# Zero products of other widths, and pooled maxima moved up, in a fused attention, bilinear and SoLU kernel

## The chip, the cores and the metric

The kernel runs on one core of a Trainium2 chip. The time is device microseconds of one execution; 735.52 us is the median of three runs (735.33 to 736.11).

The engines that matter: TensorE (PE, matrix products; loads of its stationary operand are shown as PEld), VectorE (DVE), ScalarE (ACT), GpSimd (POOL), and SyncE (SP), which issues nearly all DMAs. Each engine works through its instructions in order.

## The reference

Attention with 4 batches, 8 heads, 576 positions and head size 64 gives the sum of two parts. Its output, 2304 tokens of 512, goes through a bilinear layer and then a SoLU layer. All is fp32.

```python
def sm_attn(qq, kk, vv):
    s = scale * np.matmul(qq, kk.transpose(0, 1, 3, 2))
    s = s - np.max(s, axis=-1, keepdims=True)
    a = np.exp(s)
    a = a / (np.sum(a, axis=-1, keepdims=True) + 1e-09)
    return np.matmul(a, vv)
# pooled part: q, k, v averaged over 4 positions, attended, each row repeated 4 times
out_up = np.repeat(sm_attn(q_d, k_d, v_d), 4, axis=2)
# local part: only |i - j| < 4 counts
out_local = ...
x = out_up + out_local                # 2304 x 512
x = ((x @ w_a) * (x @ w_b)) @ w_out   # d_ff 1536
h = x @ w_in                          # d_ff 1024
solu = h * softmax(h)
out = (layernorm(solu) * g_ln) @ w_out2
```

## The kernel before

**Stages.** Tokens are taken in five blocks of 512 (the last has 256). The bilinear layer of a block runs in 12 chunks of 128 hidden columns: chunk c has a first product `A0`, a second product `A1` (12 passes each, `emit_A`), their elementwise product on DVE (`emit_mult`), its split into a high and a low half on ACT and DVE (`emit_p`), and the out product `B` (12 passes, `emit_B`), which is issued one chunk later. While a block runs, the attention of the next block is computed between its products. The attention of block 0 has no cover and runs alone at the start, some 44 us. The SoLU layer comes last.

**Splitting.** Products with 512 columns use a high and a low half of each operand, three passes for each: high x high, high x low, low x high. The weights arrive as 64-bit words and go through five steps, `w{i}.1` to `w{i}.5` (`w_stages`): two ACT instructions, a shift and an add on DVE (lines 142 and 145), a rounding on ACT (line 153), and the low half on DVE (line 160). Step 5 gives the operand of a chunk's third pass.

**Attention items.** A pooled head pair, `p{b}_{hp}`, has: sums of q and k over four positions on DVE (`qsum0`, `qsum1`, line 262), scores on PE (line 286), maxima on DVE (line 296), exponentials on ACT, normalising of E (`norm`; in block 1 all on DVE, line 335), transposes on PE (`ptr`, line 368), their copy on ACT (`pte`), the value product (`pvm`), its copy. A local unit, `l{s}` (128 tokens), has scores (line 468), maxima, exponentials (line 508), sums and scaling on DVE (`norm`, lines 517 to 528), transposes and a value product. In block 0 the local transposes are PE's (line 559); for later units DVE transposes 32 x 32 tiles (`turn32`, line 535), which SP writes to DRAM and reads back turned (`place`). Scores, transposes and value products of both kinds share the two PSUM banks `x0` and `x1`.

**Order.** For block 0 the order is written out, in `FIRST`, and is fixed on every engine. After that, items are put on a time line with `add(t, item)`, in units of which one chunk has four, and `advance(t)` issues all with a smaller time. It is called at 4c + 1.33 (between `A0` and `A1`), at 4c + 2.67 (behind the multiply) and at 4c + 4 (behind the out product of chunk c - 1). In the chunks of block 0 every engine keeps the order of issue (`pin(None)`). `p_at` and `l_at` give the times of pooled and local items of block 1 within a head pair's stretch, eight thirds of a chunk long; p1_0 to p1_3 and l4 to l7 are the items that run beside block 0's chunks.

**Zero products.** `fill` issues products of zeros into a PSUM tile that real work will overwrite. `FILL` gives how many, by place: `S0`, `S1`, `S2` ahead of the pooled scores of the first three head pairs of block 0, `pv2` ahead of the third pooled value product, `lS3`, `lPT0_0` and `lo3_0` ahead of the scores of unit 3, the first transposes of unit 0 and the value product of unit 3. All have 128 columns.

Of the kernel before, what the change touches and what calls it, by code (L numbers as in the profile page):

```python
# [17 lines left out]
B, H, S, D = 4, 8, 576, 64  # L18
# [9 lines left out]
NCH = FF1 // 128  # L28
EDGES = [8, 9, 13, 17]
NBOOT = NSUB  # L30
FILL = dict(S0=10, S1=12, S2=10, pv2=2, lPT0_0=2, lo3_0=2, lS3_0=2, PT2=0)

FIRST = (
# [25 lines left out]
def kernel(  # L59
# [17 lines left out]
    PE, ACT, DVE, POOL, SP = nc.tensor, nc.scalar, nc.vector, nc.gpsimd, nc.sync  # L77
# [106 lines left out]
    zz = base.tile([128, 128], F32, name="zz")  # L184
# [2 lines left out]
    mhalf = base.tile([128, 1], F32, name="mhalf")  # L187

    def fill(key, out):
        for _ in range(FILL.get(key, 0)):  # L190
            PE.matmul(out=out, lhsT=zz[:, 0:out.shape[0]], rhs=zz, start=True, stop=True, skip_group_check=True)


    att, att_ps = ExitStack(), ExitStack()
# [43 lines left out]
    def pooled_items(b, hp):  # L238
        i = b * NP + hp
        st = {}  # L240
# [33 lines left out]
        def scores():  # L274
            if b:
                st["S"] = [aps.tile([R, 2 * SD], F32, tag=f"x{e}", name="S") for e in range(2)]
            elif hp % 2 == 0:
                t = aps.tile([72, 2, 512], F32, tag="S", name="S")
                st["S"] = [t[:, e, 0:2 * SD] for e in range(2)]
            else:  # L280
                st["S"] = [ps.tile([72, 512], F32, tag=f"acc{e}", name="S")[:, 0:2 * SD] for e in range(2)]
            if not b:
                fill(f"S{hp}", st["S"][0][:, 0:128])
            for half in range(2):
                for e in range(2):
                    PE.matmul(
                        out=st["S"][e][:, half * SD:(half + 1) * SD],
                        lhsT=st["q"][e * 64:e * 64 + 64, half * R:half * R + R],
                        rhs=st["k"][e * 64:e * 64 + 64, :], start=True, stop=True,
                    )  # L290
# [64 lines left out]
        def ptr():  # L355
            if turned:
                return
            if b:
                st["PT"] = [aps.tile([72, 2 * SD], F32, tag=f"x{e}", name="PT") for e in range(2)]
            else:  # L360
                st["PT"] = [ps.tile([72, 512], F32, tag="ab", bufs=2, name="PT")[:, 0:2 * SD] for e in range(2)]
            if not b:
                fill(f"PT{hp}", st["PT"][0][:, 0:128])
            for e in range(2):
                for kh in range(2):
                    for h in range(2):
                        o = kh * SD + h * 72
                        PE.transpose(st["PT"][e][:, o:o + 72], st["E"][:, e, h, kh * 72:kh * 72 + 72],
                                     id_sb[:72, :72])
# [24 lines left out]
        def pve():  # L394
            if b not in up:
# [5 lines left out]
                    vsum=lambda: (vsum2(), vsum1()), smax=smax, exps=exps, norm=lambda: (inverse(), scaled()), ptr=ptr, pte=pte,  # L401
# [31 lines left out]
    def local_items(s):  # L433

        st = {}
# [13 lines left out]
        def scores(hps=range(NP)):  # L449
            if hps[0] == 0:  # L450
                if s in (1, 3):
                    t = aps.tile([128, 2, 512], F32, tag="S", name="lS")
                    st["S"] = [t[:, e] for e in range(2)]
                elif s == 2:
                    st["S"] = [ps.tile([128, 512], F32, tag=f"acc{e}", name="lS") for e in range(2)]
                else:
                    st["S"] = [aps.tile([128, 512], F32, tag=f"x{e}", name="lS") for e in range(2)]
            fill(f"lS{s}_{hps[0]}", st["S"][1][:, 384:512])
            if s < NMASK:
                for e in range(2):  # L460
                    PE.matmul(out=st["S"][e][:, 0:NP * KW].rearrange("p (h k) -> p h k", k=KW), lhsT=id_r,
                              rhs=mk_r[:, kind, :].unsqueeze(1).to_broadcast([128, NP, KW]),
                              start=True, stop=False, skip_group_check=True)
            for hp in hps:
                for n in range(2):
                    for e in range(2):
                        q, k = qk_of(n, hp, e)
                        PE.matmul(out=st["S"][e][n * QW:n * QW + QW, hp * KW:hp * KW + KW], lhsT=q, rhs=k,  # L468
                                  start=s >= NMASK, stop=True, skip_group_check=True)
# [80 lines left out]
        def ptr(half):  # L550
            def f():
                if s == 2:
                    pt_ = ps.tile([KW, 4, 128], F32, tag=f"acc{half}", name="lPT")
                else:
                    pt_ = ps.tile([KW, 4, 128], F32, tag="ab", bufs=2, name="lPT")
                fill(f"lPT{s}_{half}", pt_[:, 0, :])
                for a in range(4):
                    hp, e = 2 * half + a // 2, a % 2
                    PE.transpose(pt_[:, a, :], st["P"][:, NP * e + hp, :], id_sb)
                st["pt", half] = pt_  # L560
            return f
# [10 lines left out]
        def pvm(half):  # L572
            def f():
                if half == 0:
                    if s == 2:
                        st["o"] = aps.tile([128, 2, 512], F32, tag="S", name="lo")[:, 0].rearrange("p (h c) -> p h c", c=128)
                    else:
                        st["o"] = aps.tile([128, NP, 128], F32, tag="x0" if s == 1 else "x1", name="lo")
                fill(f"lo{s}_{half}", st["o"][:, 2 * half, :])
                for hp in (2 * half, 2 * half + 1):  # L580
                    for n in range(2):
                        for e in range(2):
                            c = (2 * hp + e) * D
                            if s > 3:
                                PE.matmul(out=st["o"][e * 64:e * 64 + 64, hp, n * QW:n * QW + QW].rearrange("p (a i) -> p a i", a=2),  # L585
                                          lhsT=st["vw"][n][:, c:c + D], rhs=st["PT"][:, 2 * n:2 * n + 2, NP * e + hp, :],
                                          start=True, stop=True, skip_group_check=True)
                                continue
                            PE.matmul(out=st["o"][e * 64:e * 64 + 64, hp, n * QW:n * QW + QW],
                                      lhsT=st["vw"][n][:, c:c + D],  # L590
                                      rhs=st["PT", half][:, 2 * (hp % 2) + e, n * QW:n * QW + QW],
                                      start=True, stop=True, skip_group_check=True)
            return f
# [12 lines left out]
        cols = slice(s % 4 * 128, s % 4 * 128 + 128)  # L606
# [488 lines left out]
    def add(t, f):  # L1095
        timeline.append((t, seq[0], f))
        seq[0] += 1
# [21 lines left out]
    for n, word in enumerate(FIRST.split()):  # L1119
        key, name = word.split(".")  # L1120
# [2 lines left out]

    QS, LS4 = 2.7, 4
    turn = 8
    p_at = dict(load=-2.5, loadv=-1, qsum0=0.95, qsum1=1.2, scores=2.8, smax=2.9, exps=3.3, vsum=3.5, norm=4.1, ptr=5.8, pte=5.9,
                pvm=6.8, pve=6.9)
    l_at = dict(loadqk=1 - turn, loadv=8.1 - turn, scores=0.8, mask=0.9, smax=0.91, exps=1.1, norm=2.1, turn32=3.4,
                place=3.45, pvm0=7.8, pvm1=7.81, evac=7.9)
# [2 lines left out]
    for blk in range(1, NBLK):  # L1132
        at = lambda r, o: 48 * (blk - 1) + (turn * r + o + (2 if blk == 1 else 0)) * 4 / 3
        for r in range(width[blk] // 128):
            if blk < B:
                for name, f in (pooled_items(blk, r) if blk > 1 else pool1[r]).items():
                    if (blk, r) == (1, 0) and "load" in name:
                        continue
                    if (blk, r) == (1, 0) and "qsum" in name:
                        add(QS + (name == "qsum1") / 100, f)  # L1140
                    else:
                        add(at(r, (q_at if blk > 1 else p_at)[name]), f)
            s = 4 * blk + r
            if s in VECTOR:
                for o, f in vector_items(s):
                    add(at(0, o + (2 + 15 * r if blk == B else turn * r - 3.7)), f)
                continue
            for name, f in locs[s].items():
                if name in l_at and not (s == 4 and "load" in name):
                    add(at(r, l_at[name] + (-0.4 if s > 7 and name == "turn32" else 0.6 if s > 7 and name == "place" else 0)) if s > 4 or l_at[name] > 1 else  # L1150
                        LS4 + l_at[name] / 100, f)
            add(at(r, 9) if blk == B else at(3, (7.2 + 0.3 * r if blk == 1 else 8 + 0.1 * r) if r < 3 else 8.3), locs[s]["split"])
    for i in range(5, 3 * NCH):
# [8 lines left out]
    def at(t, *fs):  # L1162
        for f in fs:
            late.append((t, len(late), f))
# [85 lines left out]
    blk = NBLK - 1  # L1250
# [176 lines left out]
```

## Time and profile before

| | |
|---|---|
| median of three runs | 735.52 us (735.33 to 736.11) |
| profiled execution | 742.58 us, its span 740.8 us |
| busy: PE, PEld, DVE, ACT, POOL | 722.0, 593.3, 455.3, 331.3, 241.5 us |
| instructions | 12089, of them 4478 PE passes and as many loads |
| chain that ended last | PE 68%, DVE 19%, ACT 4%, DMA 4% of the span |

A busy time is a sum over the whole span; a stage can have another limit than the sum shows. PE's share is high because nearly all stages wait for it, so what counts are the few stretches in which it stands still or runs at a lower clock. The granted clock is printed as a share of 2.4 GHz.

### The profile page before, as it was taken

To read this page: it belongs to the slowest core of one execution; us is meant where nothing else is said; L and a number is where in the kernel's file an instruction comes from. 1 tells how busy PE (TensorE), PEld (TensorE's weight loads), DVE (VectorE), ACT (ScalarE), POOL (GpSimd) and SP (SyncE) were. 2 spreads that over 40 slices of the span, in tenths; PEclk is the share of its full clock that TensorE was granted. 3 is DMA by queue.
4 is the path that set the end of the run, shared out by engine and by line. 5 is a ranking of instruction groups with operands and counts; after the bars stand their busy time and mean duration, and the time that the engine had idled before them with its cause. 6 is when DMAs were issued, how large, how long until landed. Compare 5 with 4: busy or idle time off the path is not lost.

```text
span 740.8 us, 12089 instructions
## 1 busy us (share of the span) xinstructions
PE 722.0 (97%) x4478; PEld 593.3 (80%) x4478; DVE 455.3 (61%) x874; ACT 331.3 (45%) x695; POOL 241.5 (33%) x253
## 2 busy tenths in 40 slices
PE   8898989999999999999999999999999999999997
PEld 7686767777788787887788888889898888888886
DVE  6589879887325426335425858749857865656640
ACT  5578677744122214222213111147867655544441
POOL 4410101112324423224311112110038978687332
PEclk9599999999999999999999999999999999999999
DMA  8994875336343324332231120165414554554441
GB/s 240 265 362 173 247 242 170 104 102 184 92 127 121 115 83 130 116 117 80 59 115 57 37 79 18 40 240 165 143 58 143 177 192 143 170 171 142 142 142 58
DMA packets 84275, 102.99 MB, mean 139 GB/s; under 512 B 11032, under 2 KB 65080, under 8 KB 84216
## 3 DMA queue, kind: packets, MB, share of 16 engines
q1 hardware_dynamic: 83672, 102.01, 44.2%
q8 instruction: 35, 0.57, 0.3%
q10 hardware_dynamic: 544, 0.21, 0.2%
q14 instruction: 24, 0.20, 0.1%
HBM read 75.72 MB, written 26.48 MB: 138 GB/s over the span
## 4 chain that ended last, share of the span: by engine, by line
PE 68%; DVE 19%; ACT 4%; DMA 4%; issue 3%; SPq 1%; POOL 0%; DVEq 0%; ACTq 0%; POOLq 0%
PE ab L738 24%; PE o L1083 13%; PE c L963 9%; PE acc L783 6%; PE accS L783 5%; PE c L936 3%; DVE wm L145 2%; DVE vx L687 2%; DVE vpr L685 1%; PE lo L585 1%; DVE wm L142 1%; DVE w L160 1%; PE lS L468 1%; DVE qkds L262 1%; DVE a L751 1%
## 5 line engine op out<-in xcount | busy, mean ns | idle before, releaser
L738 PE MATMUL ab<-xTh,w 128*128 128x512 f32 (+1 forms) x976 | 287.8, 369 | 4.5 <-DVE a L751 2.4
L738 PEld LDWEIGHTS ab<-xTh,w 128*128 128x128 f32 x976 | 176.4, 189 | 38.4 <-DVE w L160 3.5
L738 PE MATMUL ab<-xTl,w 128*128 128x512 f32 (+1 forms) x488 | 178.7, 366 | 0.3 <-DVE xTl L219 0.3
L738 PEld LDWEIGHTS ab<-xTl,w 128*128 128x128 f32 x488 | 92.1, 189 | 14.9 <-DVE xTl L219 1.0
L759 POOL TENSOR_TENSOR pl<-a,ph 128x512 fp32r<-128x512 f32 x36 | 47.2, 1312 | 153.9 <-ACT ph L757 153.9
L751 DVE TENSOR_TENSOR a<-a,ab 128x512 f32<-128x512 f32 (+1 forms) x60 | 37.8, 630 | 92.7 <-PE ab L738 90.3
L783 PE MATMUL acc<-ph,w 128*128 128x512 f32 (+1 forms) x288 | 88.2, 361 | 0.0
L757 ACT CAST ph<-a 128x512 fp32r<-128x512 f32 (+1 forms) x60 | 34.7, 578 | 94.7 <-DVE a L751 93.6
L746 ACT COPY a<-ab 128x512 f32<-128x512 f32 (+1 forms) x60 | 32.5, 542 | 99.5 <-PE ab L738 86.9
L268 POOL TENSOR_TENSOR vp<-vp 72x512 f32<-72x512 f32 x16 | 20.9, 1309 | 146.7 <-DMA vp<-vp 146.7
L783 PE MATMUL accS<-ph,w 128*128 128x512 f32 x192 | 66.9, 389 | 0.0
L783 PEld LDWEIGHTS acc<-ph,w 128*128 128x128 f32 x288 | 51.8, 189 | 9.3 <-issue 1.6
L1083 PE MATMUL o<-w,cTh 128*128 128x512 f32 x192 | 59.1, 389 | 0.0
L835 POOL TENSOR_TENSOR xr<-xr 128x256 f32<-128x256 f32 x28 | 29.6, 1079 | 67.7 <-DMA xr<-o1d 67.1
L783 PE MATMUL acc<-pl,w 128*128 128x512 f32 (+1 forms) x144 | 51.2, 355 | 0.0
L783 PEld LDWEIGHTS accS<-ph,w 128*128 128x128 f32 x192 | 36.0, 188 | 7.7
L1083 PEld LDWEIGHTS o<-w,cTh 128*128 128x128 f32 x192 | 36.0, 188 | 7.4
L1074 POOL TENSOR_TENSOR cTl<-raw,cTh 128x512 fp32r<-128x512 f32 x24 | 34.0, 1435 | 22.4 <-ACT cTh L1072 22.4
L145 DVE CUSTOM_DVE_ANT_0 wm<-raw,wm 128x1024 uint16<-128x1024 uint16 x52 | 37.0, 711 | 2.7
L783 PE MATMUL accS<-pl,w 128*128 128x512 f32 x96 | 37.4, 389 | 0.0
L1083 PE MATMUL o<-w,cTl 128*128 128x512 f32 x96 | 37.3, 389 | 0.0
L137 ACT ACTIVATE raw<-raw 128x512 f32<-128x512 f32 x52 | 35.7, 687 | 0.1
(168 smaller groups left out, 1248.5 us busy)
## 6 DMA issues: line engine op xcount, KB each, us to landing
raw<-w SPq DMA_DIRECT2D x52, 512.0 KB
qkr<-qkp SPq DMA_DIRECT2D x32, 288.0 KB
vd<-v SPq DMA_DIRECT2D x18, 512.0 KB
raw<-vd SPq DMA_DIRECT2D x72, 128.0 KB
vp<-vp SPq DMA_DIRECT2D x16, 288.0 KB
pd<-lT SPq DMA_DIRECT2D x12, 384.0 KB
out<-ob SPq DMA_DIRECT2D x18, 256.0 KB
vw<-vwin SPq DMA_DIRECT2D x32, 140.0 KB
```

Of the source, the lines that this page charges most:

```text
L137: ACT.activation(out=hw, in_=hw, func=AF.Prelu, scale=2.0 ** -112, alpha=2.0 ** 32)
L145: DVE.tensor_tensor(out=st["w"], in0=st["w"], in1=st["low"], op=ALU.add)
L738: PE.matmul(out=abs_[blk, j][n][:, c0:c1], lhsT=w[:, ws], rhs=x[:, k, c0:c1], start=(k == 0 and i == 0), stop=(k == 3 and i == 2), skip_gr ...
L746: ACT.copy(out=a, in_=abs_[blk, j][0])
L751: DVE.tensor_tensor(out=a, in0=a, in1=pb, op=ALU.mult)
L757: ACT.copy(out=ph, in_=a)
L759: low = lambda: (POOL if 0 < blk < NBLK - 1 else DVE).tensor_tensor(out=pl, in0=a, in1=f32(ph), op=ALU.subtract)
L783: PE.matmul(out=accs[blk][m], lhsT=wt[:, ms], rhs=x, start=(j == 0 and i == 0 and (w == WIDE or m % 2 == 0)), stop=(j == NCH - 1 and i == ...
L835: POOL.tensor_tensor(out=at[o], in0=at[m], in1=at[n], op=op)
L963: PE.matmul(out=out, lhsT=xx[:, ks], rhs=w, start=(kt == 0 and q_ == 0 and not more), stop=(kt == 1 and q_ == 2), skip_group_check=True)
L1074: POOL.tensor_tensor(out=h4(lo)[:, k], in0=raw[:, k], in1=f32(h4(hi)[:, k]), op=ALU.subtract)
L1083: PE.matmul(out=o, lhsT=x[:, k, :], rhs=w, start=(k == 0 and q_ == 0), stop=(k == 7 and q_ == 2))
```

## The change

The entries of `FILL` become pairs (number, columns). `S0` goes from 10 products of 128 columns to 28 of 48, `S1` from 12 of 128 to 12 of 64, `S2` from 10 of 128 to 4 of 256. The three places with two products of 128 columns get one of 256, and the two at `pv2` go.

In block 0's chunks the times of pooled items move: scores from 2.8 to 2.0, maxima from 2.9 to 2.05, exponentials from 3.3 to 2.4, normalising from 4.1 to 3.3. The first head pair has times of its own: scores at 7 and maxima at 7.05 (before 6.40 and 6.53), exponentials at 7.6 (before 7.07), normalising at 8.8 (before 8.13). `turn32` and `place` of units 4 to 7 go later by 0.9.

What this does to the order of issue, by item:
- p1_0: scores and maxima go from ahead of `emit_p(0, 1)` to behind the out product of chunk 0; on DVE, l4's `turn32` goes behind steps w7.5, w9.2 and w9.3, and `norm` behind `turn32`, w8.5, w10.2 and w10.3.
- p1_1 and p1_3: scores stay behind `A0`, but stand with the maxima ahead of the local unit's `norm`; exponentials and `norm` come one call of `advance` earlier and `turn32` one later.
- p1_2: scores go from behind the out product of chunk 5 to ahead of it, directly behind the second product and the multiply of chunk 6 and DVE's `qsum1`.

```diff
-FILL = dict(S0=10, S1=12, S2=10, pv2=2, lPT0_0=2, lo3_0=2, lS3_0=2, PT2=0)
+FILL = dict(S0=(28, 48), S1=(12, 64), S2=(4, 256), lS3_0=(1, 256), lPT0_0=(1, 256), lo3_0=(1, 256))
...
     def fill(key, out):
-        for _ in range(FILL.get(key, 0)):
-            PE.matmul(out=out, lhsT=zz[:, 0:out.shape[0]], rhs=zz, start=True, stop=True, skip_group_check=True)
+        if key not in FILL:
+            return
+        count, cols = FILL[key]
+        rhs = zz[:, 0:cols] if cols < 128 else zz.unsqueeze(1).to_broadcast([128, cols // 128, 128])
+        for _ in range(count):
+            PE.matmul(out=out[:, 0:cols] if cols < 128 else out.rearrange("p (a c) -> p a c", c=128)[:, 0:cols // 128], lhsT=zz[:, 0:out.shape[0]],
+                      rhs=rhs, start=True, stop=True, skip_group_check=True)
...
-    p_at = dict(load=-2.5, loadv=-1, qsum0=0.95, qsum1=1.2, scores=2.8, smax=2.9, exps=3.3, vsum=3.5, norm=4.1, ptr=5.8, pte=5.9,
+    p_at = dict(load=-2.5, loadv=-1, qsum0=0.95, qsum1=1.2, scores=2.0, smax=2.05, exps=2.4, vsum=3.5, norm=3.3, ptr=5.8, pte=5.9,
                 pvm=6.8, pve=6.9)
...
-                    if (blk, r) == (1, 0) and "qsum" in name:
+                    if (blk, r) == (1, 0) and name in ("scores", "smax", "exps", "norm"):
+                        add(dict(scores=7, smax=7.05, exps=7.6, norm=8.8)[name], f)
+                    elif (blk, r) == (1, 0) and "qsum" in name:
...
-                    add(at(r, l_at[name] + (-0.4 if s > 7 and name == "turn32" else 0.6 if s > 7 and name == "place" else 0)) if s > 4 or l_at[name] > 1 else
+                    add(at(r, l_at[name] + (dict(turn32=-0.4, place=0.6) if s > 7 else dict(turn32=0.9, place=0.9)).get(name, 0)) if s > 4 or l_at[name] > 1 else
                         LS4 + l_at[name] / 100, f)
```

The remaining lines only widen the PSUM slices that `fill` is given.

## Rows read from the trace of the kernel before

**Rows 1.** Page, parts 1 and 2: busy us (share) and instructions; clock in 40 slices

```profile
PE 722.0 (97%) x4478; PEld 593.3 (80%) x4478; DVE 455.3 (61%) x874; ACT 331.3 (45%) x695; POOL 241.5 (33%) x253
PEclk9599999999999999999999999999999999999999
```

**Rows 2.** Windows: stretch, length, busy us (instructions) by engine, granted clock, DMA share, GB/s

```profile
0.00:12.50 12.50, 11.01 (x90) 9.84 (x91) 6.24 (x14) 5.40 (x22) 2.45 (x9) 1.00 0.78 240
0.00:19.80 19.80, 16.89 (x218) 14.15 (x219) 13.39 (x31) 11.49 (x49) 9.11 (x16) 1.00 0.86 241
...
20.00:22.00 2.00, 0.38 (x8) 0.30 (x7) 0.00 (x0) 1.42 (x3) 2.00 (x3) 0.75 0.90 231
21.00:38.05 17.05, 16.37 (x142) 12.58 (x141) 10.14 (x26) 8.04 (x18) 5.68 (x7) 0.50 0.99 260
...
400.00:410.00 10.00, 10.00 (x46) 8.28 (x45) 7.36 (x13) 2.80 (x5) 2.39 (x2) 1.00 0.46 138
```

**Rows 3.** Timeline of PE: start, us, line, out<-in, count, idle before and releaser

```profile
0.99 3.82 PE L191 MATMUL S<-zz 128*72 128x128 f32 x20 [0.99 <-POOL zz L1209]
...
5.95 2.84 PE L191 MATMUL S<-zz 128*72 128x128 f32 x24
...
12.37 0.69 PE L368 MATMUL PT<-id_sb,E 72*72 72x72 f32 x8
12.90 0.40 PE L461 MATMUL lS<-mk_r,id_r 128*128 128x280 bf16 x2
...
18.35 0.68 PE L191 MATMUL lS<-zz 128*128 128x128 f32 x4 [1.31 <-DVE ss L323]
...
19.21 0.60 PE L468 MATMUL lS<-qkr 64*64 64x70 f32 x24
21.62 0.51 PE L468 MATMUL lS<-qkr 64*64 64x70 f32 x8 [1.82 <-issue]
```

**Rows 4.** DMA queues, packets, MB, share: whole span, then 18.9 to 20.2

```profile
q8 instruction: 35, 0.57, 0.3%
...
q8 instruction: 1, 0.02, 6.1%
```

**Rows 5.** Timelines of DVE, ACT and PE, three places of the first stage

```profile
7.25 1.45 DVE L262 TENSOR_REDUCE qkds<-qkr 128x144 f32<-128x576 f32 x2 [0.36 <-DMA qkr<-qkp]
...
25.74 0.82 ACT L377 COPY PTs<-PT 72x288 f32<-72x288 f32 x2 [0.38 <-PE PT L368]
...
25.92 1.15 PE L191 MATMUL pv<-zz 128*128 128x128 f32 x4
```

**Rows 6.** Timeline of PE, waits in the chunks of block 0

```profile
59.15 0.46 PE L286 MATMUL S<-qkds 64*72 64x144 f32 x2 [2.42 <-ACT lP L508]
59.99 0.71 PE L286 MATMUL S<-qkds 64*72 64x144 f32 x6 [0.38 <-ACT lP L508]
...
67.12 0.73 PE L738 MATMUL ab<-xTh,w 128*128 128x512 f32 x2 [0.27 <-DVE w L160]
...
98.66 0.67 PE L368 MATMUL PT<-id_sb,E 72*72 72x72 f32 x8 [0.56 <-DVE E L335]
...
126.66 0.67 PE L368 MATMUL PT<-id_sb,E 72*72 72x72 f32 x8 [0.78 <-DVE E L335]
```

**Rows 7.** Timeline of DVE around the first pooled head pair of block 1

```profile
62.67 0.68 DVE L160 TENSOR_TENSOR w<-wm,w 128x512 fp32r<-128x512 f32 x1
...
65.41 1.09 DVE L535 STREAM_TRANSPOSE lT<-pz 128x256 f32<-128x256 f32 x3
...
69.12 0.68 DVE L160 TENSOR_TENSOR w<-wm,w 128x512 fp32r<-128x512 f32 x1
...
70.89 0.68 DVE L751 TENSOR_TENSOR a<-a,ab 128x512 f32<-128x512 f32 x1
```

**Rows 8.** Timelines of DVE and PE at the third pooled head pair

```profile
114.84 0.75 DVE L262 TENSOR_REDUCE qkds<-qkr 128x144 f32<-128x576 f32 x1
...
116.78 0.71 PE L286 MATMUL S<-qkds 64*72 64x144 f32 x8
```

More of the change, by code (lines that the diff above doesn't have):

```diff
@@ L282, in scores @@
             if not b:
-                fill(f"S{hp}", st["S"][0][:, 0:128])
+                fill(f"S{hp}", st["S"][0][:, 0:256])
             for half in range(2):
@@ L362, in ptr @@
             if not b:
-                fill(f"PT{hp}", st["PT"][0][:, 0:128])
+                fill(f"PT{hp}", st["PT"][0][:, 0:256])
             for e in range(2):
@@ L457, in scores @@
                     st["S"] = [aps.tile([128, 512], F32, tag=f"x{e}", name="lS") for e in range(2)]
-            fill(f"lS{s}_{hps[0]}", st["S"][1][:, 384:512])
+            fill(f"lS{s}_{hps[0]}", st["S"][1][:, 0:512])
             if s < NMASK:
@@ L555, in f @@
                     pt_ = ps.tile([KW, 4, 128], F32, tag="ab", bufs=2, name="lPT")
-                fill(f"lPT{s}_{half}", pt_[:, 0, :])
+                fill(f"lPT{s}_{half}", pt_.rearrange("p a c -> p (a c)"))
                 for a in range(4):
@@ L578, in f @@
                         st["o"] = aps.tile([128, NP, 128], F32, tag="x0" if s == 1 else "x1", name="lo")
-                fill(f"lo{s}_{half}", st["o"][:, 2 * half, :])
+                fill(f"lo{s}_{half}", st["o"][:, 2 * half:2 * half + 2, :].rearrange("p a c -> p (a c)"))
                 for hp in (2 * half, 2 * half + 1):
```

## Prediction

> **What bounds the kernel now.** I read the page first, then the granted clock by stage, the timeline of TensorE (PE) up to 45 us, the DMA queues, and last PE's waits and VectorE's (DVE's) order in the first block. The page shows PE busy for 97% of the span and the granted clock at 5 tenths in one slice only, the second [rows 1]. A change pays only where it ends a wait of PE or that low clock.
>
> The windows place the low clock: 0.75 at 20 to 22 us, 0.50 (1.2 of 2.4 GHz) from 21.0 to 38.05 [rows 2]. PE is busy for 16.37 of those 17.05 us, while DVE and ScalarE (ACT) are busy for 10.14 and 8.04: there PE's speed sets the end. Ahead of the fall PE had stood still twice, 1.31 us until DVE released PSUM bank S at 18.35, and 1.82 us until 21.62 with "issue" as the reason, in the middle of 32 like products [rows 3].
>
> That second wait is for code, as I read it. Queue q8 moves instructions, 35 packets in all; PE runs 4478 + 4478 instructions [rows 1], 256 for each packet. One packet lies between 18.9 and 20.2 us, and PE goes on 1.4 us behind it [rows 3, 4]. PE stopped behind 218 + 219 = 437 instructions [rows 2]. If a packet is asked for 256 instructions ahead, this one was asked for at number 181, which is 12.5 us (90 + 91, [rows 2]), and needed 9.1 us until PE ran; the DMA engines were busy for 0.86 of the time up to there.
>
> The Trainium skill, "Runtime: NRT & Kernel Launch", section "Instruction fetch mechanics", says the same of the size (blocks of 256 instructions, the next one fetched while one runs), and that crossing a block is mostly hidden. This trace disagrees on the last point with its 1.82 us; by the page the 1.82 us would have another cause and stay, and the forecast below would be 731.8.
>
> **Zero products.** One zero product is two passes and two loads, so four instructions (10 products gave the 20 passes at 0.99, 12 the 24 at 5.95, [rows 3], and each pass has its load).
> - Ahead of the first scores: 10 products become 28, so 40 instructions become 112. A pass of 128 columns took 2.84 / 24 = 0.118 us; 48 columns take between 0.044 (by columns) and 0.066 (as the transposes of 72 columns, 8 from 12.37 to 12.90) at full clock, twice that while it is low. 20 old passes took 3.82 us, so the first three microseconds ran low; 56 new ones end between 4.7 and 6.0 us, against 5.31 for the scores, which wait for DVE. Cost 0 to 0.7; I take 0: DVE's next sum waits 0.36 for a DMA anyway [rows 5], and more than that costs its excess.
> - Second: 12 products of 64 instead of 128 columns, as many instructions, 1.4 us less work ahead of scores whose sums DVE ends at 8.70 (7.25 + 1.45, [rows 5]). Worth 0; PE then idles for some 1.2 us.
> - Third: 10 of 128 become 4 of 256, 40 instructions become 16, 0.6 us less in front of another wait. Worth 0.
> - The three single ones of 256 columns stand for two of 128: the columns and so the time are equal, with 4 instructions fewer each. The two ahead of the third pooled value product go: 1.15 us at 25.92 [rows 5] at the low clock, but that product then waits for ACT's two copies (25.74, 0.82 us, [rows 5]), so 0 to 0.5. I take 0 beside a full clock.
>
> So by the fatal place the stream is 72 - 24 - 4 = 44 instructions longer, and number 181 falls into the second scores (112 + 16 + 48 = 176 stand ahead), which run at 8.75 instead of 12.5 us. With the same delay of 9.1 us the packet is there at 17.9. PE needs it at its old number 393 (437 less 44), a few instructions into the row at 19.21, whose 24 passes and 25 loads ended the 437 [rows 3]. The spare is 1.3 us: the stall of 1.82 goes, PE stands still only until 18.35, and I expect the clock to stay at 2.4 GHz.
>
> Then the stretch: 16.37 us of work at half clock become 8.2, saving 8.2. Waits that the slow PE had covered come up, estimated from ACT's 0.82 for two copies [rows 5]: the third value product behind two copies 0.9, the first local transposes 0.3, two local value products behind one copy each 0.35; together 1.9. The next packet is asked for at about 18.9 and with 9.1 us is there at 28.0, where PE would be at 26.5 to 28: I take 1.0. Sum of the stage: 1.82 + 8.2 - 1.9 - 1.0 = 7.1 gained. Bounds: 0 if nothing changes, 10.0 if neither waits nor packet cost anything.
>
> **Block 0, first pooled head pair.** Its scores move behind the out product of chunk 0. Before, PE waited 2.42 + 0.38 us for them and 0.27 us for a weight [rows 6]. Now 12 out passes fill that wait (0.22 us each: 46 in 10 us of dense work, [rows 2], so 2.6), the scores start at the same 59.99 and end at 60.6. But the next product's third pass needs the weight remainder that DVE ends at 63.35 (62.67 + 0.68, [rows 7]); so PE waits some 2.3 us there; ten passes then end at 65.55 and the next twelve at 68.2. Before, the third of those twelve stood until 67.12 [rows 6], and the last ended at 67.12 + 10 x 0.22 = 69.3, 1.1 us later. There the transposes want the normalised E. DVE has no gap in this stretch. Its block transposes (65.41 to 66.42) go behind a weight, and E, ended at 69.12 before, now goes behind them and three weight steps (69.12 to 70.89, 1.77 us, [rows 7]): it ends at about 70.89, where the multiply began. PE's transposes start at about 70.95 instead of 69.5: **1.4 us lost**. Bounds: 1.1 gained if DVE is earlier by chance, 2.0 lost. SP's queue: the block's write and three reads go a stage later, ahead of the same weight load as before (in pairs 1 to 3 one load now passes them); PE reads the block about a chunk later, so 0. ACT's exponentials change places with two weight steps, with nobody waiting; POOL's order stays.
>
> **The other three.** Head pairs 1 and 3 keep their place on PE; DVE takes their maxima ahead of the local sums, where it may wait for PE (0 to 0.5), and E comes a stage earlier: pair 1 saves its wait of 0.56 [rows 6]. Together I take a gain of 0.6. Pair 2's scores move ahead of an out product. They need DVE's second sum, which stands behind the multiply and ends at 115.59 (114.84 + 0.75, [rows 8]); the product ahead of them ends 12 passes before the old scores, at 116.78 - 2.6 = 114.1. PE waits 1.5, where before the out product covered it. The wait of 0.78 for E [rows 6] goes: 0.7 lost. Sum of block 0: 1.4 - 0.6 + 0.7 = **1.5 us lost**, bounds 0.5 gained to 3 lost.
>
> **Sum.** The profiled execution took 742.58 us, span 740.8 and 1.8 around it. 742.58 - 7.1 + 1.5 = 737.0. The median of the timed runs is 735.52, so 7.06 below; the same step gives **729.9, say 730.0**. Its own range is 726.5 to 733.
>
> **Rivals.**
> - *Timed runs never lost the clock.* For: they are 7.06 us shorter, close to the 8.2 - 1.9 = 6.3 that the low clock costs. Against: their spread of 0.8 us needs no second cause, and no row says that the DMA engines have less to do without a profile. Then the change is the stall (1.8) against block 0 (1.5): 735.3.
> - *The clock falls again.* For: PE was busy for 96% of the low stretch and the clock still rose only at 38.05, so this mix of small products and transposes may not hold it; if it falls where the local transposes begin, half of the work from 21.62 to 28.2 (3.3) and the stall remain, less 1.0 of waits: 4.1 gained, 1.5 lost, 733.0. Against: transposes and scores of the same kind from 12.37 on ran at full clock. The Trainium skill, "TensorE: Matmul & The Clock Gate", section "Part 4: PE-mode transpose", says that transposes don't count as PE being busy for the clock; the low stretch, busy with them for about a third, agrees.
> - *Slower: E is late and nothing pays for it.* The place is the transposes at 69.5; from the point where E ends later than that each 0.1 costs 0.1. If the packet still lands at 20.2 (DMA has worked off its loads only then) or costs the timed runs nothing, block 0 stands alone: 735.5 + 1.5 = 737.0.
> - *Slower: the thinner second products lose the clock at once.* PE idles 1.2 us at 7.5 to 8.75. If the clock falls behind it, PE's work from 11.7 to 16.9, about 5 us, takes twice as long, of which about 4 show: 739.5. Against: the idle 1.31 alone, up to 18.35, left the clock at full at first.
>
> **How the numbers follow.** Forecast 0.33, never lost 0.25, falls again 0.14, E late 0.18, clock lost at once 0.10. The range 726.5 to 738.5 leaves out the last case and small tails. About 0.2% (1.5 us) is what a measurement of this kernel can tell from no change. Faster by more: the forecast, most of "falls again" and a little of "never lost", 0.48; within: the rest of "never lost" and parts of the next, 0.26; slower: 0.26.
>
> **What would show it.** Right: no "issue" wait of PE at 18 to 22 us, a q8 packet before 18, granted clock 1.00 from 18 to 38, the first half-width product at 37 instead of 44.11; then a wait for E ahead of the first pooled transposes and one for a sum ahead of pair 2's scores. Wrong: the clock at 0.50 in the same stretch, or block 0 (from the first product to the end of its chunk 11) no longer than before.

## The result, and the profile after

The change makes the kernel slower: 741.85 us (four runs, 741.59 to 743.00) against 735.82 (four runs, 735.33 to 736.19), a ratio of 1.0085 [1.0068, 1.0103]. The forecast was 730.0 with a range of 726.5 to 738.5. The profiled execution of after took 741.59 us, its span 739.8. Of the 240 timed runs behind the ratios and estimates below, the five above 749 us are left out of both.

The page of after, where the low clock of [rows 1] is gone from the second slice:

```profile
PE 720.5 (97%) x4492; PEld 591.9 (80%) x4492; DVE 453.5 (61%) x874; ACT 331.3 (45%) x695; POOL 242.9 (33%) x253
PEclk9999999999999999999999999999999999999999
```

Windows of after (columns as in [rows 2]):

```profile
0.00:12.50 12.50, 11.51 (x96) 10.92 (x96) 3.87 (x8) 3.44 (x12) 1.49 (x9) 1.00 0.82 235
...
21.00:38.05 17.05, 15.33 (x256) 11.66 (x258) 16.01 (x38) 14.89 (x38) 9.21 (x10) 1.00 0.97 273
66.40:69.80 3.40, 3.40 (x9) 2.63 (x9) 3.37 (x7) 2.98 (x6) 0.00 (x0) 0.50 0.85 276
114.20:117.60 3.40, 3.40 (x9) 2.63 (x9) 3.26 (x11) 1.96 (x10) 0.00 (x0) 0.50 1.06 385
```

From 21.00 to 38.05 PE now does 256 passes, where it did 142 at half clock [rows 2]. The half clock is in two short stretches of block 0 instead (66.40 and 114.20). And it is at the start: the window prints 1.00 there because the trace's clock record begins only with the first rise, at 11.79 us (at 3.92 in the trace of before). What the clock was ahead of that, the durations tell. Timeline of PE in after (zero products are line 195 now, pooled scores 291, transposes of E 373, bilinear products 743):

```profile
0.99 6.95 PE L195 MATMUL S<-zz 128*72 128x48 f32 x56 [0.99 <-POOL zz L1216]
7.87 1.24 PE L291 MATMUL S<-qkds 64*72 64x144 f32 x8
9.04 3.02 PE L195 MATMUL S<-zz 128*72 128x64 f32 x24
11.99 0.71 PE L291 MATMUL S<-qkds 64*72 64x144 f32 x8
...
21.56 0.67 PE L195 MATMUL lS<-zz 128*128 128x256 f32 x2 [1.31 <-DVE ss L328]
...
38.71 0.38 PE L743 MATMUL ab<-xTh,w 128*128 128x256 f32 x1
...
58.00 0.73 PE L743 MATMUL ab<-xTh,w 128*128 128x512 f32 x2 [2.05 <-DVE w L160]
65.70 0.67 PE L373 MATMUL PT<-id_sb,E 72*72 72x72 f32 x8 [2.40 <-DVE E L340]
93.11 0.73 PE L743 MATMUL ab<-xTh,w 128*128 128x512 f32 x2 [1.41 <-DVE w L160]
112.47 0.82 PE L291 MATMUL S<-qkds 64*72 64x144 f32 x8 [1.61 <-DVE qkds L267]
```

Three things are to be seen. The first zero products take 6.95 us, the scores behind them 1.24 instead of the 0.71 of later ones, and the first scores start at 7.87, not 5.31 [rows 3]; by the products of unit 3's scores (21.56, before 18.35) the stream is 3.2 us late. There is no "issue" wait at 18 to 24 us any more, and the first half-width product (the first bilinear product, 256 columns) starts at 38.71, 5.40 earlier than in before's profile:

```profile
44.11 0.39 PE L738 MATMUL ab<-xTh,w 128*128 128x256 f32 x1
```

Then block 0 gives 5.1 of those 5.40 back (like products of block 1 run 0.33 earlier), at waits of 2.05, 2.40, 1.41 and 1.61 us and in the two stretches at half clock, each of which begins within 1.8 us behind one of the waits. The end is 1.0 us earlier than in before's own profile, but that profile was 7.06 us above the median of its timed runs.

The packet of code, in a DMA view of 17.2 to 18.6 us of after (it lay between 18.9 and 20.2 before, [rows 4]):

```profile
q8 instruction: 1, 0.02, 5.8%
```

DVE in after, around the first pooled pair and the third:

```profile
57.26 0.69 DVE L160 TENSOR_TENSOR w<-wm,w 128x512 fp32r<-128x512 f32 x1
...
61.65 1.09 DVE L540 STREAM_TRANSPOSE lT<-pz 128x256 f32<-128x256 f32 x3
62.66 0.65 DVE L160 TENSOR_TENSOR w<-wm,w 128x512 fp32r<-128x512 f32 x1
...
64.80 0.75 DVE L340 TENSOR_TENSOR E<-E,ss 72x576 f32<-72x576 f32 x1
...
111.58 0.75 DVE L267 TENSOR_REDUCE qkds<-qkr 128x144 f32<-128x576 f32 x1
```

E ends at 65.55 (64.80 + 0.75), behind the block transposes and a weight's steps, and the second sum of the third pair at 112.33: the two waits of PE above.

### The profile page after: what moved, and what is told of

It is laid out like the page before. It is cut to its first block, busy times and chain, and to the rows that moved or that the text cites. A ratio compares the mean times of both kernels' runs of the same rounds, so it can differ in the third digit from the quotient of the medians.

```text
span 739.8 us, 12117 instructions
## 1 busy us (share of the span) xinstructions
PE 720.5 (97%) x4492; PEld 591.9 (80%) x4492; DVE 453.5 (61%) x874; ACT 331.3 (45%) x695; POOL 242.9 (33%) x253
## 4 chain that ended last, share of the span: by engine, by line
PE 73%; DVE 17%; ACT 4%; DMA 3%; issue 2%; SPq 0%; DVEq 0%; ACTq 0%; POOL 0%; POOLq 0%
PE ab L743 27%; PE o L1088 13%; PE c L968 9%; PE acc L788 7%; PE accS L788 6%; PE c L941 3%; DVE vx L692 2%; DVE wm L145 2%; PE lo L590 2%; DVE vpr L690 2%; PE S L195 1%; DVE a L756 1%; PE S L291 1%; DVE w L160 1%; PE lS L473 1%
## 5 line engine op out<-in xcount | busy, mean ns | idle before, releaser
L788 PE MATMUL accS<-ph,w 128*128 128x512 f32 x192 | 68.2, 396 | 0.0
L840 POOL TENSOR_TENSOR xr<-xr 128x256 f32<-128x256 f32 x28 | 27.6, 1005 | 67.9 <-DMA xr<-o1d 67.3
L1079 POOL TENSOR_TENSOR cTl<-raw,cTh 128x512 fp32r<-128x512 f32 x24 | 35.9, 1515 | 22.6 <-ACT cTh L1077 22.6
```

Source lines behind the costliest of these rows:

```text
L788: PE.matmul(out=accs[blk][m], lhsT=wt[:, ms], rhs=x, start=(j == 0 and i == 0 and (w == WIDE or m % 2 == 0)), stop=(j == NCH - 1 and i == ...
L840: POOL.tensor_tensor(out=at[o], in0=at[m], in1=at[n], op=op)
L1079: POOL.tensor_tensor(out=h4(lo)[:, k], in0=raw[:, k], in1=f32(h4(hi)[:, k]), op=ALU.subtract)
```

## The experiments

Two questions: why does after not have the 7 us that its profile should save, and what makes it slower? Theory A: the timed runs of before hadn't the long half clock of its profile; the first zero products and the new order each cost time, and the terms add up. Theory B: the half clock is in every run, and something else eats the gain. Each kernel is compared with runs of before on the same chip; ratios are of those. A run's time hangs on how often the clock falls in it: over 235 runs, in 17 sets of one kernel each, the time within a set goes by 0.54 us for each 0.001 of mean granted clock (one slope by least squares; that mean leaves out the time ahead of the first rise). "At full clock" below is an estimate, the mean of the times less that share, good to 0.2 to 0.5 us.

**The kernel before, once more** (no edit).

> The kernel before, unchanged. Theory A (its timed runs never lost the clock at 21 us, its one profile did): 735.8 us again, within 0.2%; granted clock of a timed run 0.99 or more; in the profile the first half-width product starts at 35 to 38 us (44.11 in the first profile) and no granted clock of 0.50 lies between 21 and 38 us. Theory B (the low stretch is in every run of this kernel): the profile shows 0.50 from about 21 to 38 us again and the product at about 44.

737.81 us (736.06 to 749.39), ratio 0.9987 [0.9952, 1.0022]. Windows of its profile, then PE's timeline:

```profile
21.00:38.05 17.05, 16.08 (x262) 13.30 (x262) 15.45 (x34) 13.81 (x29) 5.84 (x6) 1.00 0.99 259
54.50:57.90 3.40, 3.40 (x9) 2.63 (x10) 3.30 (x10) 2.93 (x6) 0.00 (x0) 0.50 1.04 422
92.00:95.40 3.40, 3.40 (x13) 2.56 (x12) 2.92 (x7) 2.36 (x5) 0.00 (x0) 0.51 0.48 130
```

```profile
21.17 0.35 PE L468 MATMUL lS<-qkr 64*64 64x70 f32 x8 [0.69 <-issue]
...
52.87 0.46 PE L286 MATMUL S<-qkds 64*72 64x144 f32 x2 [2.33 <-ACT lP L508]
```

The same program, and the 17 us at half clock aren't there: 262 passes in the window where [rows 2] has 142. The code stall is 0.69 instead of 1.82. The falls lie elsewhere and are short. Theory B is out: the long stretch is not in every run. Half clock of that amount isn't rare, though: of 118 timed runs of before with a clock on record, 27 have a mean of 0.988, the profile's own, or less; where in the run it lay isn't on record. Theory A's time was off by 2 us, and one run had a mean clock of 0.975 where A asked for 0.99 or more: it left the falls out. In four sets of 17 to 31 runs the kernel before had medians of 738.09 to 739.32, single runs from 734.87 up, and 735.15 to 735.5 at full clock.

**The new zero products, old order.**

```diff
-FILL = dict(S0=10, S1=12, S2=10, pv2=2, lPT0_0=2, lo3_0=2, lS3_0=2, PT2=0)
+FILL = dict(S0=(28, 48), S1=(12, 64), S2=(4, 256), lS3_0=(1, 256), lPT0_0=(1, 256), lo3_0=(1, 256))
...
```

> The kernel before with the new zero products alone, the old order in block 0. Theory A: the 56 narrow passes keep the clock at half until about 11.8 us (3.9 in the first profile of before), and everything behind them comes 3.2 us later, the first half-width product at about 38.7: 735.8 + 3.2 = 739.0 us. Theory B: the first stage gains what its profile showed, 44.11 - 38.71 = 5.4 us: 730.4 us.

738.64 us, ratio 1.0014 [0.9999, 1.0029]; at full clock 737.0. Theory B's 730.4 is far off. Theory A's 739.0 is near the median, in part by luck, since it had no falls in it: at full clock the cost is 1.7, not 3.2. The first zero products took 6.96 us again.

**The new order, old zero products.**

```diff
-    p_at = dict(... scores=2.8, smax=2.9, exps=3.3, vsum=3.5, norm=4.1, ...)
+    p_at = dict(... scores=2.0, smax=2.05, exps=2.4, vsum=3.5, norm=3.3, ...)
...
+                        add(dict(scores=7, smax=7.05, exps=7.6, norm=8.8)[name], f)
...
```

> The kernel before with the new order in block 0 alone, the old zero products. Theory A: the order costs by itself, 1.5 us of waits for E and the second sum, and up to 1.7 us for each of two falls of the clock behind those waits (near 63 and 112 us): 737.3 us without falls, 739 with both. Theory B (the order is not what costs): within 0.2% of 735.8 us.

740.80 us, ratio 1.0039 [1.0009, 1.0069]; at full clock 737.1. PE in its profile, where the clock had fallen at 56.59:

```profile
57.52 1.22 PE L738 MATMUL ab<-xTh,w 128*128 128x512 f32 x2 [2.05 <-DVE w L160]
...
65.40 0.67 PE L368 MATMUL PT<-id_sb,E 72*72 72x72 f32 x8
```

The transposes don't wait for E here: E ended at 65.08, and PE, at half clock, came to them at 65.40. A late E and a clock fall in front of it cover each other. The time is above both theories (739 at most), by the falls: the mean clock of its runs was 0.992.

**After, with the first zero products of before.**

```diff
-FILL = dict(S0=(28, 48), ...
+FILL = dict(S0=(10, 128), ...
```

> The changed kernel with the first zero products as before, 10 of 128 columns. Theory A: the clock rises at 3 to 5 us again, the first pooled scores start at 5.3 instead of 7.87 us, and the whole is about 3.2 us faster than the changed kernel: 738.6 us. Theory B: no change against 741.85 us, since the first scores wait for their DMA and sums anyway.

738.50 us, as Theory A had it (738.6), ratio 0.9996 [0.9965, 1.0026]; at full clock 736.0. PE at the start:

```profile
0.99 4.54 PE L195 MATMUL S<-zz 128*72 128x128 f32 x20 [0.99 <-POOL zz L1216]
5.46 1.17 PE L291 MATMUL S<-qkds 64*72 64x144 f32 x8
6.55 1.77 PE L195 MATMUL S<-zz 128*72 128x64 f32 x24
```

The second zero products, the same 24 passes, take 1.77 us here and 3.02 in after: 0.074 and 0.126 us each, at full clock and, but for the end, at half.

**After, once more**, on the chip of the next experiment and of the two headed "E early".

> The changed kernel once more, to stand beside the other kernels of this job. Theory A (the loss adds up: narrow first zero products hold the clock at half and end 3.2 us later; the new order adds a wait of 2.4 for the normalised E and one of 1.6 for the second sum, with clock falls behind them): 741.5 to 742.5, about 3.3 above the kernel with the first zero products back (738.5), the first zero products again some 7 us long at 0.123 us a pass, the half clock until 11 to 12 us. Theory C (the 741.85 was the chance place of the clock falls in four runs): 738 to 740, with runs spread over 5 us or more as those of the kernel before.

741.63 us (740.39 to 744.06), ratio 1.0037 [1.0012, 1.0061]; at full clock 738.9, which is 2.8 above the kernel with the first zero products back. The wait for E was 0.80, behind a clock fall at 58.29. Its line, and the window of 40 to 70 us (columns as in [rows 2]), where DVE is busy for 28.06 of the 30.00:

```profile
65.76 0.67 PE L373 MATMUL PT<-id_sb,E 72*72 72x72 f32 x8 [0.80 <-DVE E L340]
...
40.00:70.00 30.00, 26.82 (x166) 20.81 (x166) 28.06 (x57) 24.82 (x57) 0.55 (x1) 0.94 0.82 309
```

The loss stands, and chance (Theory C) is out: the lowest of ten runs is above the highest that C allowed. The loss is smaller in the ratio than at first, since there the four runs of before lay within 0.9 us of its full-clock time, here their median is 738.11.

**Fewer narrow products first**: 18 of 48 columns.

```diff
-FILL = dict(S0=(28, 48), ...
+FILL = dict(S0=(18, 48), ...
```

> The changed kernel with 18 instead of 28 first zero products of 48 columns: 36 passes by 0.123 us are 4.4 us, as long as 20 passes of 128 columns at half clock. Theory A1 (narrow passes don't raise the clock): the half clock lasts beyond 8 us although the fill ends at 5.4, and the second zero products run at half clock too (about 0.126 a pass); first scores end at 6.7, third head pair's scores at about 13 to 13.5 against 11.84 with wide products; 739.5 to 740.5. Theory A2 (any stream of passes raises it after some microseconds; 28 were only too many): clock at full at 4 to 7 us, second zero products at 0.074 a pass, 738.5 as with wide products.

740.88 us, ratio 1.0047 [1.0016, 1.0077]; at full clock 738.0.

```profile
0.99 4.55 PE L195 MATMUL S<-zz 128*72 128x48 f32 x36 [0.99 <-POOL zz L1216]
5.47 1.24 PE L291 MATMUL S<-qkds 64*72 64x144 f32 x8
6.64 3.14 PE L195 MATMUL S<-zz 128*72 128x64 f32 x24
9.71 1.15 PE L291 MATMUL S<-qkds 64*72 64x144 f32 x8
10.79 1.95 PE L195 MATMUL S<-zz 128*72 128x256 f32 x8
```

The fill ends when that of 128 columns does (4.55 and 4.54 us), but the second zero products still run at half clock, 0.131 us each; the record of the clock begins at 10.64. So the number wasn't the fault: Theory A2 is out.

**The kernel before with narrow first products alone.**

```diff
-FILL = dict(S0=10, ...
+FILL = dict(S0=28, ...
...
+            n = 48 if key == "S0" else 128
+            PE.matmul(out=out[:, 0:n], ..., rhs=zz[:, 0:n], ...)
```

> The kernel before with one edit: 28 first zero products of 48 columns. Theory A: first scores at 7.9 instead of 5.4, half clock until the second zero products (128 columns here) have run for some microseconds, 10 to 12 us; 2.5 to 3 above the kernel before, 740.6 to 741.1. Rival (the late start is taken back at the waits of block 0, which before has at other times): 738.1 to 738.6.

740.58 us, ratio 1.0009 [0.9986, 1.0032]; at full clock 737.9, 2.6 above before's 735.3. By the ratio alone this is inconclusive: the clock fell more often in the runs of before beside it (mean clock 0.993, against 0.996). The 2.6 is Theory A's (2.5 to 3), and so is its start, with the first scores at 7.88 and the clock's first rise at 11.68:

```profile
0.99 6.96 PE L192 MATMUL S<-zz 128*72 128x48 f32 x56 [0.99 <-POOL zz L1210]
7.88 1.24 PE L287 MATMUL S<-qkds 64*72 64x144 f32 x8
9.05 4.11 PE L192 MATMUL S<-zz 128*72 128x128 f32 x24
13.09 0.71 PE L287 MATMUL S<-qkds 64*72 64x144 f32 x8
```

**The other new zero products alone**, old order.

```diff
-FILL = dict(S0=10, S1=12, S2=10, pv2=2, lPT0_0=2, lo3_0=2, lS3_0=2, PT2=0)
+FILL = dict(S0=(10, 128), S1=(12, 64), S2=(4, 256), lS3_0=(1, 256), lPT0_0=(1, 256), lo3_0=(1, 256))
...
```

> The kernel before with the new zero products everywhere but in the first place, which keeps 10 of 128 columns; old order. Theory A (terms add up; the other new fills were worth 1.0 at equal clock between the kernels with old fills and new order, and with first fill back): 1.0 below the kernel before, 737.1. Rival (fills behind the first are all beside a wait and cost and bring nothing): as the kernel before, 738.1.

736.93 us, ratio 0.9975 [0.9950, 1.0000]; at full clock 735.3, as before. So the rival has it, and not Theory A's gain of 1.0. The median is the lowest without the new order, and the kernel is clearly faster than after; against before, only its fewer falls (mean clock 0.996) show.

The three edits together, as they were combined:

| first | others | order | ratio to before | at full clock |
|---|---|---|---|---|
| old | old | old | 0.9987 [0.9952, 1.0022] | 735.3 |
| narrow | old | old | 1.0009 [0.9986, 1.0032] | 737.9 |
| old | new | old | 0.9975 [0.9950, 1.0000] | 735.3 |
| old | old | new | 1.0039 [1.0009, 1.0069] | 737.1 |
| narrow | new | old | 1.0014 [0.9999, 1.0029] | 737.0 |
| old | new | new | 0.9996 [0.9965, 1.0026] | 736.0 |
| narrow | new | new | 1.0037 [1.0012, 1.0061] | 738.9 |

Narrow first products cost 2.6, 1.6 and 2.8 (lines that differ in them alone), the order 1.8, 0.7 and 1.9, the other fills 0.0, -0.9 and -1.0: means of 2.3, 1.5 and -0.7, sum 3.1 of the 3.5 measured. A single difference is good to some 0.5 us, so that the other fills' share isn't told from nothing.

**E early**: the first fill back, and the first pair's normalising ahead of the block transposes.

```diff
-add(dict(scores=7, smax=7.05, exps=7.6, norm=8.8)[name], f)
+add(dict(scores=7, smax=7.05, exps=7.6, norm=8.2)[name], f)
...
```

> The changed kernel with 10 first zero products of 128 columns, and the first head pair's normalising issued at 8.2 instead of 8.8, so ahead of the block transposes of l4 and of three weight steps on DVE. Theory A: the wait of 2.40 for E at 63.65 goes; the median falls from 738.5 by 2.4, to 736.1, and by up to 1.7 more if the clock fall behind that wait (64.45 to 67.86) goes too. Theory D (DVE has no gap in this stretch, so that the work put behind E makes PE wait as long at the next place): 738.5, with a new wait of about 2 us for a weight or a multiply between 60 and 75 us.

737.94 us, ratio 0.9985 [0.9953, 1.0017]; at full clock 735.5, only 0.5 under the kernel without this edit, not 2.4. Timelines of DVE, ACT and PE, and then the view of line 396 (durations in ns, the semaphore's in the last row):

```profile
63.78 1.08 DVE L540 STREAM_TRANSPOSE lT<-pz 128x256 f32<-128x256 f32 x3
...
65.81 0.69 DVE L145 CUSTOM_DVE_ANT_0 wm<-raw,wm 128x1024 uint16<-128x1024 uint16 x1
...
66.59 0.62 ACT L153 CAST w<-wm 128x512 fp32r<-128x512 f32 x1 [1.78 <-DVE wm L145]
...
68.25 0.66 ACT L382 COPY PTs<-PT 72x288 f32<-72x288 f32 x2
...
68.72 0.95 PE L396 MATMUL pv<-PTs,vp 72*64 72x144 f32 x8 [1.19 <-issue]
```

```profile
L396 PEldq EVENT_SEMAPHORE  x1: 4445/4445/4445, 64.2 to 64.2; - x1
```

The wait for E is gone, and 1.19 of it is back one step later. The timeline says "issue", but PE's queue stood at a semaphore (4.4 us from 64.2): ACT's copy of PT stood behind a weight's rounding, which waited for DVE's shift, which stood behind E, the block transposes and two weight steps.

**E early, and the third pair's scores behind the out product.**

```diff
+                    elif (blk, r, name) == (1, 2, "scores"):
+                        add(at(r, 2.01), f)
...
```

> As the one before, and the third head pair's scores behind the out product again (at 2.01 instead of 2.0 in its stretch). Theory A: the wait of 1.6 for the second sum at 110.4 goes as well: 1.6 below the one before, 734.5 (up to 1.7 less with a clock fall). Theory D: no change from the one before, the wait comes up as one for E or a weight within the next chunk.

737.97 us, ratio 0.9999 [0.9976, 1.0023]; at full clock 735.3.

```profile
89.43 0.74 PE L743 MATMUL ab<-xTh,w 128*128 128x512 f32 x2 [1.95 <-DVE w L160]
...
114.91 0.73 PE L743 MATMUL ab<-xTh,w 128*128 128x512 f32 x2 [0.96 <-DVE w L160]
```

The wait of 1.6 went; one of 0.96 for a weight came, and the one before it is 1.95 instead of 1.36. From the trace with only the first fill back, the end comes 1.5 us earlier, not 4.0. Theory D holds for the larger part.

**Weights first**: in block 0 the local sums and scaling (2.0 us on DVE) behind the weight that the next product needs.

```diff
+                    elif (blk, r, name) == (1, 1, "norm"):
+                        add(18.01, f)
...
+                    if blk == 1 and name == "norm":
+                        add((8.21, 18.02, 27.34, 38.01)[r], f)
+                        continue
...
```

> As the kernel with the first zero products back, E early and the third pair's scores behind the out product, and in block 0 DVE does a chunk's weight remainder (step 5) ahead of the local unit's sums and scaling (2.0 us): l4's go behind E of the first pair (8.21), l5's and the second pair's E behind w15.5 (18.02 and 18.01), l6's to 27.34, l7's to 38.01. Theory A (each wait of PE in block 0 is an order on DVE): the waits for a weight in the trace of the kernel without this edit (2.05, 1.95, 0.96, 0.67, 0.25, sum 5.9) go, some 1 to 2 come back as waits for E; 733 to 735, some 4 us under the kernel before. Theory D (DVE's work in block 0 is the bound, whatever its order): 737 to 738, waits for E or a multiply in place of those for weights.

740.62 us, ratio 1.0017 [0.9992, 1.0042]; at full clock 738.4, 3.1 above the kernel without this edit and above both theories. Theory A is wrong at this place:

```profile
65.70 0.62 ACT L153 CAST w<-wm 128x512 fp32r<-128x512 f32 x1 [3.94 <-DVE wm L145]
...
67.34 0.67 ACT L382 COPY PTs<-PT 72x288 f32<-72x288 f32 x2
...
67.81 1.47 PE L396 MATMUL pv<-PTs,vp 72*64 72x144 f32 x8 [3.28 <-issue]
```

The same chain, longer by the local sums: ACT idles 3.94 and PE 3.28. PE's clock fell in that wait, at 67.54, for 6.8 us.

**The block transposes later**: E early, third pair back, and l4's transposes behind the next weight steps.

```diff
+                    if (s, name) in ((4, "turn32"), (4, "place")):
+                        add(8.7 + (name == "place") / 100, f)
+                        continue
...
```

> As the kernel with the first zero products back, E early and the third pair's scores behind the out product; besides, the block transposes of l4 (and their DMAs) go from 8.40 to 8.70, so on DVE behind the steps w8.5, w10.2 and w10.3. In the kernel with E early alone, PE waited 1.19 (no releaser named) for the first pair's value product: ACT's copy of PT stood behind a weight rounding that waited 1.78 for DVE's shift, and DVE had E and the block transposes (1.09) ahead of that shift. Theory E (that chain turned the removed wait into a new one): the shift comes 1.1 earlier, ACT's idle time falls to 0.7 and PE's wait to under 0.3; the time is 0.5 to 1.1 below that of the kernel without this edit (0.9999 of the kernel before), so 0.9985 to 0.9992 of the kernel before. Theory D (DVE's total work sets the pace): the wait comes up as one for E, a weight or a multiply, 1.0000 of the kernel before.

737.24 us, ratio 0.9972 [0.9943, 1.0000]; at full clock 735.6, no better than without the edit. The ratio is below both theories', but the clock also fell less in these runs (mean 0.997) than in those of before beside them (0.993).

```profile
64.45 0.60 ACT L153 CAST w<-wm 128x512 fp32r<-128x512 f32 x1
```

The rounding runs without a wait, and PE doesn't wait for the value product; but PE ran at half clock from 56.80 to 63.63 in that profile and came late anyway. Whether the chain is cut in a run without that fall stays open.

## Why the prediction was wrong

The forecast was a gain of 5.5 us (735.52 to 730.0); it is a loss of 6.0.

- **The step that failed first: carrying the profile's gain to the timed runs** ("the same step gives 729.9"). The 7.06 between the profile and the median was, but for little, the half clock itself, so it was subtracted twice: once as a stretch that the change removes, once as the distance to the timed runs. The run without it shows that the kernel does without the stretch; that the four timed runs of before did is read from their times (735.33 to 736.19 beside 735.3 at full clock), as their clock isn't on record. The rival "never lost the clock" read the timed runs rightly; it was given 0.25 on the argument that a spread of 0.8 us needs no second cause, where the fact that a known stretch explains 6.3 of 7.06 was the stronger one.
- **The stage itself gained what was forecast, in part by luck.** There was no stall, and the clock was full from 21.00 to 38.05. The waits that the slow PE had covered came to 1.1 (1.9 forecast), and the next packet cost nothing (1.0 forecast). The first product came at 38.71, 1.7 behind the forecast 37 with a start 3.2 late. The packet came at 17.4 to 18.7 (forecast 17.9), but not by the working given: instruction 181 ran at 12.0 us and not at 8.75, so that the delay of 9.1 would have put PE's going on at 21.1. There was room all the same, because PE, late by its start, came to number 437 only at 22.4. In the 14 traces the packet ends 4.3 to 7.7 us behind that instruction, so no fixed delay is shown. In three more traces there is a stall, of 0.69, 1.11 and 1.23 us, and it ends 1.3 to 1.5 behind the packet, as the 1.4 of before; in traces whose packet ended by 19.5 there was none. The Trainium skill's "mostly hidden" ("Runtime: NRT & Kernel Launch", "Instruction fetch mechanics") doesn't hold in those four. The rival "the clock falls again" found nothing in the trace of after: transposes, like the rest, ran at 1.00 in this stretch. The Trainium skill's rule on transposes ("TensorE: Matmul & The Clock Gate", "Part 4: PE-mode transpose") is not decided by that, since other products stand between them; in the low stretch of before they took 7.2 of the 17.05 us (2.35 pooled, 4.80 local), more than the third that was read. But in five of the twelve later traces the clock fell at 19.0 to 23.5 us, for 3.4 or 6.8 us, beside waits of 1.1 to 1.3.
- **The first zero products were mis-sized**: cost 0 (bounds 0 to 0.7), measured 1.6 to 2.8 us by the estimate at full clock. The step "56 new ones end between 4.7 and 6.0 us" took for granted that the clock rises after the first three microseconds, whatever PE runs. A pass of 48 columns took 0.123 us all along, near the upper bound of 0.066 doubled, and none ran at full clock. The nearest rival, thinner second products that lose the clock (739.5), had the time nearest the result (2.4 short), but by luck, not by the mechanism: the clock wasn't lost there, it hadn't come.
- **Block 0 was sized well**: 1.5 forecast, 0.7 to 1.9 measured by the estimate at full clock. In the profile of after, the wait for a weight came as 2.05 (2.3 forecast), for the second sum as 1.61 (1.5), and E was the late one, at 2.40 (2.75, from 68.2 to 70.95). That this profile shows 5.1 lost and not 1.5 fits its two falls, by estimate up to 1.7 each.
- **The second and third zero products and the rest**: 0 forecast, 0.0 to -1.0 measured.
- **What no term had**: clock falls in the timed runs. The four of after had mean clocks of 0.992 to 0.998 and lay some 2.7 us above the estimate at full clock (739.1 for that set); before's four lay 0.5 above theirs, which was luck: its later sets lie 2.6 to 4.0 above, by their medians. So the 6.0 is more than the change costs; by the estimates at full clock it costs 3.5.

So of the 11.85 us between forecast and result, about 6.4 are the gain that the timed runs didn't have to give (7.1 less the 0.7 of the other fills, which is itself uncertain), 2.3 the narrow first products, and 2.2 (2.7 less 0.5) the falls; the remaining 1 isn't assigned.

## What to carry to other kernels

Before a gain is booked from one profiled execution, ask whether the timed runs have the stretch at all: where the profile is longer than their median by about what the stretch costs, the two are one thing. Where an engine is busy for over nine tenths of a stage (the second profile of after has DVE at 28.06 of the 30.00 us from 40 to 70), moving an item may only move the wait, and not only along that engine: follow the chain through the next queue, here DVE's shift, ACT's rounding, ACT's copy, PE. A warm-up fill is judged by what its passes take and by when the work behind it reaches its full-clock duration, not by its columns.

## What was not expected of the hardware

The clock's first rise is at 3.92 to 6.71 us in the nine traces with 128-column first products, and at 10.50 to 11.79 in the five with 48-column ones, of 36 as of 56 passes. The Trainium skill ("TensorE: Matmul & The Clock Gate", "Part 1: The HAM clock gate") says that the slow start is a matter of time and not of the number of matrix products; here time alone didn't do it, since PE was busy from 0.99 us on in both. What of width, loads or the scores behind them brought the rise stays open.

Of 23 falls of the clock in the 14 traces (the one at the very end, when PE is done, not counted), each lies in a wait of PE of 1.1 us or more or within 1.8 us behind its end, but not every such wait has one (the 2.42 of [rows 6] has none). Most lasted 3.4 us, some 6.8 and one 17.1; by estimate a short one costs up to 1.7 us where PE sets the pace. With the slope above (0.54 us for each 0.001 of mean clock), this fits that runs of the kernel before lie anywhere from 735 to 751 us. If the waits bring the falls, a wait in front of PE can cost more than its length; that they do isn't shown.
